# Last cross layer of the last 1024 rows with rows on partitions: column-tiled matmuls, sums added by identity matmuls, one multiply-add per 128 rows

## Chip, cores and metric

One core of a Trainium2 chip. The metric is the device time of one execution in microseconds (us). "Span" is the time from the first to the last instruction in a profile; the timed figure is some 1.75 us longer. Most runs agree within a few tenths; some are 1.5 to 2.5 us longer. Those over 1.5% above the kernel's fastest run are called slow and left out of ratios.

## The reference

```python
# x0: (4096, 416), ws: (6, 416, 416), bs: (6, 416), all bf16
x = x0
for l in range(6):
    x = x0 * (x @ ws[l] + bs[l]) + x
```

Since every layer adds onto x, x after layer l is x0 * (1 + sum of all (x @ ws + bs) so far). The kernel keeps this sum in PSUM and never resets it between the layers of one group of rows.

## The kernel before

Four superblocks of 1024 rows pass through six layers each. Features lie on partitions, rows on the free dimension. 416 features are three chunks of 128 and a tail of 32. TensorE works in four column tiles of 128x32 side by side for the chunks, and in row tiles for the tail. VectorE evicts each PSUM bank with one multiply:

```python
for half in range(2):            # 512 rows each
    ...
    for c in range(NC):          # three chunks of 128 features
        ...
        dve.scalar_tensor_tensor(
            out=dst, in0=ps[:, NC * half + c, :], scalar=cb_sb[:, c, l:l + 1],
            in1=x0T_sb[:, c, o:o + H], op0=ALU.add, op1=ALU.mult,
        ).then_inc((s_xa, s_xb)[half], 1)
```

`cb_sb` holds one plus the sum of biases, per feature. The result has features on partitions, but the output wants rows. Superblocks 0 to 2 are turned by DMA transposes, hidden behind the next superblock. The last one has nothing behind it, so it is turned on TensorE, copied by ScalarE and VectorE and stored in pieces; the last two stores (208 KB each) are released at the same moment:

```python
def out_chunk(c):                # first 512 rows: identity matmuls
    for j in range(4):
        for q in range(4):
            ins = tile_mm(ps[lane(q), c, j * 128:j * 128 + 128],
                xo_sb[:, NS - 1, c, j * 128 + 32 * q:j * 128 + 32 * q + 32], ident[:, :], q, True)
...
# rows 512 to 1023: transposes, then copies by VectorE and ScalarE
...
sp.wait_ge(s_oeD, 2)
sp.wait_ge(s_oet, 1)
sp.dma_start(out_v[:, j + 6:j + 8, :], o_sb[:, j + 6:j + 8, :]).then_inc(s_out, 16)
...
act.wait_ge(s_oet, 1)
act.wait_ge(s_oeA, 4)
act.wait_ge(s_oeD, 1)
act.dma_start(out_v[:, j0 + 4:j0 + 6, :], o_sb[:, j0 + 4:j0 + 6, :]).then_inc(s_out, 16)
```

## Time and profile before

| | |
|---|---|
| time | 131.05 us median of 3 runs (130.9 to 131.08) |
| span of the profiled run | 130.5 us, a slow run of 132.34 us |
| one layer of one superblock | 4.87 us |
| last VectorE copy to the end of the span | 3.17 us |

The page gives busy shares and the chain that ended last; the chain of waits in order of time shows the tail; the timeline gives durations. The prediction shows these lines.

### The profile page before, as it was taken

Reading aid. Unit: us, or ns where it says so; the run is one execution under the profiler, and the core shown is the slowest. Engines: PE = TensorE matmul, PEld = TensorE weight load, DVE = VectorE, ACT = ScalarE, POOL = GpSimd, SP = SyncE. Lnnn points to the kernel's source line nnn. Section 1 sums busy time; section 2 is a strip of 40 time slices with the busy share of each in tenths; the row PEclk is TensorE's granted clock in tenths of the full one; section 3 lists DMA queues with packets and bytes.
Section 4 is the critical chain, followed back from the end, with each engine's and each line's share of the span. In section 5 each row is a group of like instructions: output and inputs, shape, how many; then the busy total and the mean of one; then the engine's idle time right before and its main releaser. Section 6 shows DMA issues by size and latency. Waiting matters only on the chain.

```text
span 130.5 us, 5378 instructions
## 1 busy us (share of the span) xinstructions
PE 125.8 (96%) x2436; PEld 62.9 (48%) x2436; DVE 100.3 (77%) x154; ACT 71.5 (55%) x163; POOL 22.6 (17%) x41
## 2 busy tenths in 40 slices
PE   7999999999999999999999999999999999999980
PEld 5555445445445445445445445445445445445450
DVE  2427797797797797797798798798788788788780
ACT  0623563575763564575764564575754554554670
POOL 7502022022022023022022023022022023022140
PEclk9999999999999999999999999999999999999997
DMA  3963099900008979800006699700008900700026
GB/s 99 312 152 90 13 228 219 173 5 0 5 5 58 207 93 203 274 23 5 0 5 132 135 123 204 260 6 0 5 0 49 211 12 0 261 6 5 3 76 190
DMA packets 32882, 12.54 MB, mean 96 GB/s; under 512 B 25302, under 2 KB 32860, under 8 KB 32860
## 3 DMA queue, kind: packets, MB, share of 16 engines
q1 hardware_dynamic: 31356, 11.37, 42.9%
q10 hardware_dynamic: 1312, 0.78, 2.1%
q8 instruction: 19, 0.31, 1.0%
q0 software_dynamic: 192, 0.06, 0.2%
q14 instruction: 3, 0.02, 0.1%
HBM read 2.90 MB, written 3.41 MB: 48 GB/s over the span
## 4 chain that ended last, share of the span: by engine, by line
PE 93%; DMA 3%; DVE 1%; SPq 0%; issue 0%; DVEq 0%
PE ps L211 82%; PE ps L350 10%; DMA xin_sb<-in_x_dram 3%; PE ps L261 1%; DVE xo_sb L458 1%; DVE o_sb L463 0%; SPq L121 0%; DVEq L33 0%; PE ps L366 0%
## 5 line engine op out<-in xcount | busy, mean ns | idle before, releaser
L458 DVE SCALAR_TENSOR_TENSOR xT_sb<-ps,cb_sb,x0T_sb 128x512 bf16<-128x512 f32 x120 | 80.8, 743 | 16.6 <-PE ps L350 16.6
L211 PE MATMUL ps<-xT_sb,w_sb 128*32 128x512 bf16 (+1 forms) x1680 | 89.0, 364 | 0.0
L211 PEld LDWEIGHTS ps<-xT_sb,w_sb 128*32 128x32 bf16 x1680 | 43.0, 97 | 38.7 <-issue 4.2
L485 ACT ACTIVATE xt_sb<-xt_sb 32x256 bf16<-32x256 bf16 x80 | 33.1, 414 | 16.7 <-POOL xt_sb L198 16.0
L505 ACT ACTIVATE t_sb<-ps,cb_sb 64x256 f32<-64x256 f32 x48 | 22.5, 470 | 30.4 <-PE ps L211 30.1
L198 POOL TENSOR_TENSOR xt_sb<-t_sb,x0t_sb 128x256 bf16<-128x256 f32 x20 | 13.5, 674 | 85.9 <-ACT t_sb L505 85.9
L211 PE MATMUL ps<-x0T_sb,w_sb 128*32 128x512 bf16 (+1 forms) x336 | 19.8, 383 | 0.0
L458 DVE SCALAR_TENSOR_TENSOR xo_sb<-ps,cb_sb,x0T_sb 128x512 bf16<-128x512 f32 x23 | 15.6, 744 | 3.7 <-PE ps L350 3.3
L211 PEld LDWEIGHTS ps<-x0T_sb,w_sb 128*32 128x32 bf16 x336 | 8.9, 101 | 8.3 <-issue 2.1
L350 PE MATMUL ps<-xt_sb,wt_sb 32*128 32x512 bf16 x80 | 12.1, 379 | 0.0
L518 ACT ACTIVATE x0t_sb<-x_sb 32x256 bf16<-32x256 bf16 x24 | 9.9, 413 | 0.4
L366 PE MATMUL ps<-xt_sb,wt_sb 32*128 32x512 bf16 x40 | 7.8, 385 | 0.0
L350 PE MATMUL ps<-xt_sb,wc_sb 32*128 32x256 bf16 x80 | 7.7, 268 | 0.0
L350 PEld LDWEIGHTS ps<-xt_sb,wt_sb 32*128 32x128 bf16 x80 | 2.3, 92 | 8.5 <-DVE xT_sb L458 8.5
L350 PEld LDWEIGHTS ps<-xt_sb,wc_sb 32*128 32x128 bf16 x80 | 4.0, 93 | 2.3
L198 POOL TENSOR_TENSOR xot_sb<-t_sb,x0t_sb 128x256 bf16<-128x256 f32 x4 | 2.7, 674 | 12.6 <-ACT t_sb L505 12.6
L211 PE MATMUL ps<-const-bfloat16-1.0 128*32 128x256 bf16 x44 | 2.7, 416 | 0.8 <-PEq L556 0.8
L440 DVE CAST x0T_sb<-ps 128x256 bf16<-128x256 f32 x2 | 0.8, 425 | 3.2 <-PE ps L211 3.2
L480 ACT ACT_TABLE_LOAD x1 | 1.3, 1283 | 3.6 <-issue 3.6
L350 PE MATMUL ps<-x0t_sb,wt_sb 32*128 32x512 bf16 x16 | 2.4, 379 | 0.0
L489 ACT ACTIVATE x0t_sb<-ps 128x512 bf16<-128x512 f32 x1 | 0.6, 597 | 3.1 <-PE ps L211 3.1
L211 PEld LDWEIGHTS ps<-const-bfloat16-1.0 128*32 128x32 bf16 x44 | 1.8, 138 | 1.1 <-issue 0.8
(43 smaller groups left out, 32.0 us busy)
## 6 DMA issues: line engine op xcount, KB each, us to landing
out_dram<-o_sb SPq DMA_DIRECT2D x3, 832.0 KB, 4.1
w_sb<-in_ws_dram SPq DMA_DIRECT2D x5, 312.0 KB, 4.5
xin_sb<-in_x_dram SPq DMA_DIRECT2D x2, 208.0 KB, 3.7
w_sb<-in_ws_dram ACTq DMA_DIRECT2D x1, 312.0 KB, 3.8
out_dram<-o_sb SPq DMA_DIRECT2D x1, 256.0 KB, 2.7
xin_sb<-in_x_dram ACTq DMA_DIRECT2D x1, 208.0 KB, 2.8
out_dram<-o_sb SPq DMA_DIRECT2D x1, 208.0 KB, 2.2
out_dram<-o_sb ACTq DMA_DIRECT2D x1, 208.0 KB, 2.7
```

The lines of the kernel that those rows point to most:

```text
L198: pool.tensor_tensor(out=dst, in0=t32_sb[:, n % 2, :], in1=x0t_sb[:, s, 0:G], op=ALU.mult).then_inc(s_xt, 1)
L211: return pe.matmul(dst, lhsT=lhsT, rhs=rhs, start=start, stop=True, skip_group_check=True, tile_position=(0, 32 * q),)
L261: ins = pe.transpose(out=psT[:, IN_BANKS[h][c], (j % 2) * 128:(j % 2 + 1) * 128], in_=xin_sb[:, j, c * 128:(c + 1) * 128], identity=ident[ ...
L350: return pe.matmul(dst, lhsT=lhsT, rhs=srct[lane(g), cols], start=l == 0 and start, stop=True, skip_group_check=True, tile_position=(32 * ...
L366: pe.matmul(ps[:, NC * h + 2, :], lhsT=wt_sb[lane(g), l, 0:128], rhs=srct[lane(g), :].rearrange("p (b r) -> p b r", b=2)[:, ::-1, :], star ...
L440: dve.tensor_copy(out=x0T_sb[:, c, 512:768], in_=ps[:, THIRD[c], 0:G]).then_inc(s_inD, 1)
L458: dve.scalar_tensor_tensor(out=dst, in0=ps[:, NC * half + c, :], scalar=cb_sb[:, c, l:l + 1], in1=x0T_sb[:, c, o:o + H], op0=ALU.add, op1= ...
L480: act.activation(out=x0T_sb[:, 1, h * 256:(h + 1) * 256], in_=psT[:, IN_BANKS[h][1], 0:256], func=ACTF.Copy).then_inc(s_inA, 1)
L485: ins = act.activation(out=buf[lane(g), G:2 * G], in_=buf[lane(g ^ 1), 0:G], func=ACTF.Copy)
L489: act.activation(out=x0t_sb[:, 0, :], in_=ps[:, 5, :], func=ACTF.Copy).then_inc(s_te, 1)
L505: ins = act.activation(out=t32_sb[HALVES[h], n % 2, :], in_=tail(h), func=ACTF.Identity, bias=cb_sb[HALVES[h], NC, l:l + 1],)
L518: ins = act.activation(out=x0t_sb[lane(g), s + 1, swap * G:(swap + 1) * G], in_=x4_sb[96:128, s, r * G:(r + 1) * G], func=ACTF.Copy,)
```

## The change

Intent: compute the last layer of the last superblock directly with rows on partitions. The activations become the weights of the column tiles (32 rows each), and the layer's weight matrix streams through with 416 columns. No transpose and no copy is left at the end: one VectorE multiply-add per 128 rows writes the output tile. The price is that the sums of layers 0 to 4, which lie in PSUM the other way round, must be copied to bf16 and added by identity matmuls. Core of the diff, cut:

```diff
+            def nat_tile(t):
+                for k in range(NC):
+                    if k == 0 and t < 3:
+                        pe.wait_ge(s_xa, NC * (NL - 1))
+                        pe.wait_ge(s_q, t + 1)
+                    for q in range(4):
+                        tile_mm(
+                            ps[lane(q), NAT_BANKS[t], 0:D], xT_sb[:, (L - 1) % 2, k, t * 128 + 32 * q:t * 128 + 32 * q + 32],
+                            w_sb[:, L - 1, k, :], q, t < 3 and k == 0,
+                        )
+            def nat_sums(t):
+                ...      # 3 chunks x 4 column tiles: sums of the layers before, times the identity
+            nat_tile(0)
+            nat_tile(1)
+            pe.wait_ge(s_q, NC)
+            nat_sums(0)
+            nat_sums(1)
+            nat_tile(2)
+            nat_sums(2)
+            ...
             for r in range(2):
+                pe.wait_ge(s_xb, NC * (NL - 1) - (2, 0)[r])
+                pe.wait_ge(s_q, NC + 1 + r)
+                if r == 1:
+                    pe.wait_ge(s_qD, 1)
+                ...      # tail features: 4 row-tiled matmuls, 4 identity matmuls of 32 columns
+            ins.then_inc(s_nt, 3)
+            for t in range(3, JS):
+                nat_tile(t)
+                nat_sums(t).then_inc(s_nt, 1)
...
+            for t in range(JS):
+                dve.wait_ge(s_nt, max(t + 1, 3))
+                dve.scalar_tensor_tensor(
+                    out=o_sb[:, j0 + t, :], in0=ps[:, NAT_BANKS[t], 0:D], scalar=1.0,
+                    in1=x0n_sb[:, t, :], op0=ALU.add, op1=ALU.mult,
+                ).then_inc(s_o, 1)
...
+            for j in (2, 6):      # ScalarE's queue; (0, 4) on SyncE's
+                act.wait_ge(s_o, j + 2)
+                act.dma_start(out_v[:, j0 + j:j0 + j + 2, :], o_sb[:, j0 + j:j0 + j + 2, :]).then_inc(s_out, 16)
```

ScalarE makes five of the six bf16 copies of sums (`s_q` counts them), VectorE the last (`s_qD`), and POOL the tail's.

More of the change, by code (lines that the diff above doesn't have):

```diff
@@ L49, in bass_standalone__dcn_v2_cross__recsys_kernel @@
         t32_sb = sb("t32_sb", [128, 2, G], FP32)
-        a32_sb = sb("a32_sb", [128, H], FP32)
+        x0n_sb = sb("x0n_sb", [128, JS, D])
+        wl_sb = sb("wl_sb", [128, D])
         xo_sb = sb("xo_sb", [128, NS, NC, SB])
@@ L59, in bass_standalone__dcn_v2_cross__recsys_kernel @@
         cb_sb = sb("cb_sb", [128, NC + 1, L], FP32)
+        cq_sb = sb("cq_sb", [128, NC + 2], FP32)
         ps = es.enter_context(nc.psum_tensor("ps", [128, 8, 512], FP32))
@@ L77, in bass_standalone__dcn_v2_cross__recsys_kernel @@
         s_xa, s_xb = sem("s_xa"), sem("s_xb")
-        s_a32, s_xaP = sem("s_a32"), sem("s_xaP")
+        s_cq, s_q, s_qD, s_qt = sem("s_cq"), sem("s_q"), sem("s_qD"), sem("s_qt")
+        s_x0n, s_wl, s_nt = sem("s_x0n"), sem("s_wl"), sem("s_nt")
         s_ta, s_xt, s_sw = sem("s_ta"), sem("s_xt"), sem("s_sw")
         s_oT, s_ot, s_otc = sem("s_oT"), sem("s_ot"), sem("s_otc")
-        s_pA, s_pB, s_pt, s_out = sem("s_pA"), sem("s_pB"), sem("s_pt"), sem("s_out")
-        s_oet, s_oeA, s_oeD = sem("s_oet"), sem("s_oeA"), sem("s_oeD")
+        s_out, s_o = sem("s_out"), sem("s_o")
         x0_v = x0.rearrange("(j p) d -> p j d", p=128)
@@ L96, in bass_standalone__dcn_v2_cross__recsys_kernel @@
         THIRD = (3, 6, 7)
+        NAT_BANKS = (0, 1, 2, 6, 7, 4, 3, 5)
         HALVES = (slice(0, 64), slice(64, 128))
@@ L103, in tail @@
             return ps[HALVES[h], 6 + h, 0:G]
+        j0 = (NS - 1) * JS
         def load_wt(eng, g, a, b, done):
@@ L145, in _ @@
                     load_rows(s + 2)
+                if s == 0:
+                    for g in range(4):
+                        sp.dma_start(wl_sb[lane(g), :], ws[L - 1, DF:D, :]).then_inc(s_wl, 16)
+                if s == 1:
+                    sp.dma_start(x0n_sb[:, :, :], x0_v[:, (NS - 1) * JS:NS * JS, :]).then_inc(s_x0n, 16)
                 sp.wait_ge(s_oT, 16 * NC * (s + 1))
@@ L150, in _ @@
                 ).then_inc(s_out, 16)
-            j = (NS - 1) * JS
-            sp.wait_ge(s_oeA, 2)
-            sp.dma_start(out_v[:, j:j + 4, 0:256], o_sb[:, j:j + 4, 0:256]).then_inc(s_out, 16)
-            sp.wait_ge(s_oeA, 3)
-            sp.wait_ge(s_oet, 1)
-            sp.dma_start(out_v[:, j:j + 4, 256:D], o_sb[:, j:j + 4, 256:D]).then_inc(s_out, 16)
-            sp.wait_ge(s_oeD, 2)
-            sp.wait_ge(s_oet, 1)
-            sp.dma_start(out_v[:, j + 6:j + 8, :], o_sb[:, j + 6:j + 8, :]).then_inc(s_out, 16)
+            for j in (0, 4):
+                sp.wait_ge(s_o, j + 2)
+                sp.dma_start(
+                    out_v[:, j0 + j:j0 + j + 2, :], o_sb[:, j0 + j:j0 + j + 2, :]
+                ).then_inc(s_out, 16)
             sp.wait_ge(s_out, 16 * (NS + 3))
@@ L191, in _ @@
                     if n == NL:
-                        pool.wait_ge(s_a32, 1)
+                        break
+                    if n == 1:
+                        pool.tensor_scalar(
+                            out=cq_sb[:, 0:NC + 1], in0=cb_sb[:, :, L - 1], scalar1=-1.0, scalar2=None, op0=ALU.add
+                        ).then_inc(s_cq, 1)
+                        pool.wait_ge(s_cq, 1)
                         pool.tensor_tensor(
-                            out=xo_sb[:, s, 2, 0:H], in0=a32_sb[:, :], in1=x0T_sb[:, 2, s * SB:s * SB + H], op=ALU.mult
-                        ).then_inc(s_xaP, 1)
+                            out=cq_sb[:, NC + 1:NC + 2], in0=cq_sb[:, NC:NC + 1], in1=cb_sb[:, NC, L - 2:L - 1], op=ALU.subtract
+                        ).then_inc(s_cq, 1)
                     pool.wait_ge(s_ta, n)
@@ L200, in _ @@
                     ).then_inc(s_xt, 1)
+                    if n == NL - 1:
+                        pool.tensor_scalar(
+                            out=xot_sb[:, s, :], in0=t32_sb[:, n % 2, :], scalar1=cq_sb[:, NC + 1:NC + 2], scalar2=None, op0=ALU.add
+                        ).then_inc(s_qt, 1)
                     if l == 2 and s > 0:
@@ L265, in _ @@
                 ins.then_inc(s_inT, 1)
-            def out_chunk(c):
-                for j in range(4):
-                    for q in range(4):
-                        ins = tile_mm(
-                            ps[lane(q), c, j * 128:j * 128 + 128],
-                            xo_sb[:, NS - 1, c, j * 128 + 32 * q:j * 128 + 32 * q + 32], ident[:, :], q, True,
-                        )
-                ins.then_inc(s_pA, 1)
             for s in range(NS):
@@ L278, in _ @@
                     n = s * L + l
-                    last = n == NL - 1
+                    if n == NL - 1:
+                        break
                     if l == 0:
@@ L388, in _ @@
                         chunk(m, 1).then_inc(s_mb, 1)
-                        if last and m < 2:
-                            pe.wait_ge(s_xa, NC * (NL - 1) + m + 1)
-                            out_chunk(m)
-                            if m == 1:
-                                pe.wait_ge(s_xaP, 1)
-                                out_chunk(2)
-            pe.wait_ge(s_xt, NL)
-            pe.wait_ge(s_xb, NC * NL - 2)
-            for r in range(2):
-                for q in range(4):
-                    c = r * 128 + 32 * q
-                    ins = tile_mm(ps[lane(q), 3, r * 128:r * 128 + 128], xot_sb[:, NS - 1, c:c + 32], ident[:, :], q, True)
@@ L402, in _ @@
-            ins.then_inc(s_pt, 1)
-            def out_transposes(c, j, bank, slot):
-                return pe.transpose(
-                    out=psT[:, bank, slot * 128:(slot + 1) * 128],
-                    in_=xo_sb[:, NS - 1, c, j * 128:(j + 1) * 128], identity=ident[:, :],
-                )
-            pe.wait_ge(s_xb, NC * NL - 1)
-            for jj in range(4):
-                for c in range(2):
-                    ins = out_transposes(c, 4 + jj, 4, jj * 2 + c)
-            ins.then_inc(s_pB, 1)
@@ L415, in _ @@
-            pe.wait_ge(s_xb, NC * NL)
-            pe.wait_ge(s_oeA, 1)
-            for jj in range(4):
-                ins = out_transposes(2, 4 + jj, (5, 0)[jj // 2], jj % 2)
-                if jj % 2:
-                    ins.then_inc(s_pB, 1)
-        j0 = (NS - 1) * JS
+            def nat_tile(t):
[8 more added lines that the diff above has]
+                        )
@@ new lines, in nat_sums @@
+            def nat_sums(t):
+                for c in range(NC):
+                    for q in range(4):
+                        ins = tile_mm(
+                            ps[lane(q), NAT_BANKS[t], c * 128:c * 128 + 128],
+                            xo_sb[:, NS - 1, c, t * 128 + 32 * q:t * 128 + 32 * q + 32], ident[:, :], q, False,
+                        )
+                return ins
+            nat_tile(0)
+            nat_tile(1)
+            pe.wait_ge(s_q, NC)
+            nat_sums(0)
@@ new lines, in _ @@
+            nat_sums(1)
+            nat_tile(2)
+            nat_sums(2)
+            pe.wait_ge(s_xt, NL - 1)
+            pe.wait_ge(s_qt, 1)
+            pe.wait_ge(s_wl, 64)
+            for r in range(2):
+                pe.wait_ge(s_xb, NC * (NL - 1) - (2, 0)[r])
+                pe.wait_ge(s_q, NC + 1 + r)
+                if r == 1:
+                    pe.wait_ge(s_qD, 1)
+                for g in range(4):
+                    t, rows = 2 * g + r, slice(r * 128, r * 128 + 128)
+                    pe.matmul(
+                        ps[:, NAT_BANKS[t], 0:D], lhsT=xt_sb[lane(g), (L - 1) % 2, rows], rhs=wl_sb[lane(g), :],
+                        start=t >= 3, stop=True, skip_group_check=True, tile_position=(32 * g, 0),
+                    )
+                for g in range(4):
+                    t, rows = 2 * g + r, slice(r * 128, r * 128 + 128)
+                    ins = pe.matmul(
+                        ps[:, NAT_BANKS[t], DF:D], lhsT=xot_sb[lane(g), NS - 1, rows], rhs=ident[lane(g), lane(g)],
+                        start=False, stop=True, skip_group_check=True, tile_position=(32 * g, 0),
+                    )
@@ L444, in _ @@
                     n = s * L + l
+                    if n == NL - 1:
+                        break
                     for half in range(2):
@@ L447, in _ @@
                             dve.wait_ge(s_ti, n + 1)
-                        for c in range(NC):
-                            if n == NL - 1 and half == 0 and c == 2:
-                                continue
+                        for c in (1, 0, 2) if n == NL - 2 and half == 0 else range(NC):
+                            if n == NL - 2 and half == 0 and c == 0:
+                                dve.wait_ge(s_q, 1)
                             if half == 1:
@@ L461, in _ @@
                             ).then_inc((s_xa, s_xb)[half], 1)
-            dve.wait_ge(s_pB, 1)
-            dve.tensor_copy(
-                out=o_sb[:, j0 + 4:j0 + 8, 0:256], in_=psT[:, 4, :].rearrange("p (j d) -> p j d", d=256)
-            ).then_inc(s_oeD, 1)
-            dve.wait_ge(s_pB, 3)
-            dve.tensor_copy(
-                out=o_sb[:, j0 + 6:j0 + 8, 256:DF], in_=psT[:, 0, 0:256].rearrange("p (j d) -> p j d", d=128)
-            ).then_inc(s_oeD, 1)
+            dve.wait_ge(s_cq, 1)
+            dve.tensor_scalar(
+                out=xo_sb[:, NS - 1, 2, H:SB], in0=ps[:, NC + 2, :], scalar1=cq_sb[:, 2:3], scalar2=None, op0=ALU.add
+            ).then_inc(s_qD, 1)
+            dve.wait_ge(s_x0n, 16)
+            for t in range(JS):
[4 more added lines that the diff above has]
+                ).then_inc(s_o, 1)
         @block.scalar
@@ L486, in swap_lanes, with previous_sums @@
                 ins.then_inc(done, 1)
+            def previous_sums(half, c):
+                act.activation(
+                    out=xo_sb[:, NS - 1, c, half * H:(half + 1) * H], in_=ps[:, NC * half + c, :],
+                    func=ACTF.Identity, bias=cq_sb[:, c:c + 1],
+                ).then_inc(s_q, 1)
             act.wait_ge(s_tp, 1)
@@ L496, in _ @@
                     if n == NL:
+                        break
+                    if n == NL - 1:
+                        act.wait_ge(s_cq, 1)
                         act.wait_ge(s_ti, n)
-                        act.activation(
-                            out=a32_sb[:, :], in_=ps[:, 2, :], func=ACTF.Identity, bias=cb_sb[:, 2, l:l + 1],
-                        ).then_inc(s_a32, 1)
+                        previous_sums(0, 0)
+                        act.wait_ge(s_xa, NC * (n - 1) + 1)
+                        previous_sums(0, 1)
                     act.wait_ge(s_to, n)
@@ L509, in _ @@
                     ins.then_inc(s_ta, 1)
-                    if l < L - 1:
+                    if n == NL - 1:
+                        act.wait_ge(s_xa, NC * n)
+                        previous_sums(0, 2)
+                        for c in range(2):
+                            act.wait_ge(s_xb, NC * (n - 1) + c + 1)
+                            previous_sums(1, c)
+                    elif l < L - 1:
                         act.wait_ge(s_xt, n)
@@ L523, in _ @@
                             ins.then_inc(s_te, 1)
-            for c in range(NC):
-                act.wait_ge(s_pA, c + 1)
-                act.activation(
-                    out=o_sb[:, j0:j0 + 4, c * 128:c * 128 + 128],
-                    in_=ps[:, c, :].rearrange("p (j d) -> p j d", d=128), func=ACTF.Copy,
-                ).then_inc(s_oeA, 1)
-            act.wait_ge(s_pt, 1)
-            act.activation(
-                out=o_sb[:, j0:j0 + JS, DF:D].rearrange("p (g r) f -> p r g f", r=2),
-                in_=ps[:, 3, 0:256].rearrange("p (r g f) -> p r g f", g=4, f=DR), func=ACTF.Copy,
-            ).then_inc(s_oet, 1)
-            act.wait_ge(s_pB, 2)
-            act.activation(
-                out=o_sb[:, j0 + 4:j0 + 6, 256:DF], in_=psT[:, 5, 0:256].rearrange("p (j d) -> p j d", d=128), func=ACTF.Copy
-            ).then_inc(s_oeA, 1)
-            act.wait_ge(s_oet, 1)
-            act.wait_ge(s_oeA, 4)
-            act.wait_ge(s_oeD, 1)
-            act.dma_start(out_v[:, j0 + 4:j0 + 6, :], o_sb[:, j0 + 4:j0 + 6, :]).then_inc(s_out, 16)
+            for j in (2, 6):
+                act.wait_ge(s_o, j + 2)
+                act.dma_start(
+                    out_v[:, j0 + j:j0 + j + 2, :], o_sb[:, j0 + j:j0 + j + 2, :]
+                ).then_inc(s_out, 16)
 _INS = ['x0', 'ws', 'bs']
```

## The prediction

> **What bounds the kernel now.** I read the page first: busy shares, then the chain that ended last.
>
> ```profile
> PE 125.8 (96%) x2436; PEld 62.9 (48%) x2436; DVE 100.3 (77%) x154; ACT 71.5 (55%) x163; POOL 22.6 (17%) x41
> ...
> PE 93%; DMA 3%; DVE 1%; SPq 0%; issue 0%; DVEq 0%
> ```
>
> TensorE carries 93% of the chain. The change touches only the end, so next I took the chain of waits from 100 us on, in order of time. Columns: start, length, what.
>
> ```profile
> 117.21 0.32 PE ps L350
> ...
> 117.76 4.33 PE ps L211 x84
> 122.08 0.32 PE ps L350
> ...
> 122.63 3.13 PE ps L211 x96
> 125.76 0.03 issue
> 125.79 0.75 DVE xo_sb L458
> 126.54 0.60 DVE o_sb L463
> 127.14 0.20 DVEq L33
> ```
>
> One layer of one superblock is 122.08 - 117.21 = 4.87 us. The last layer follows: TensorE until 125.76, one VectorE multiply, copies, and the stores. The span ends at 130.5, so 3.1 us after the last copy are DMA and the end of the program. Then the timeline of these stretches:
>
> ```profile
> 117.83 4.04 DVE L458 SCALAR_TENSOR_TENSOR xT_sb<-ps,cb_sb,x0T_sb 128x512 bf16<-128x512 f32 x6 [0.83 <-PE ps L350]
> 118.25 0.95 ACT L505 ACTIVATE t_sb<-ps,cb_sb 64x256 f32<-64x256 f32 x2 [1.44 <-PE ps L211]
> 119.28 0.68 POOL L198 TENSOR_TENSOR xt_sb<-t_sb,x0t_sb 128x256 bf16<-128x256 f32 x1 [4.19 <-ACT t_sb L505]
> ...
> 122.70 0.69 ACT L498 ACTIVATE a_sb<-ps,cb_sb 128x512 f32<-128x512 f32 x1 [1.02 <-PE ps L350]
> ...
> 123.55 0.40 PE L211 MATMUL ps<-ident,xo_sb 128*32 128x128 bf16 x16
> ...
> 123.77 0.82 PE L211 MATMUL ps<-xT_sb,w_sb 128*32 128x512 bf16 x12
> ...
> 124.42 0.67 PE L211 MATMUL ps<-ident,xo_sb 128*32 128x128 bf16 x32
> ...
> 127.36 0.37 SPq L159 DMA_DIRECT2D out_dram<-o_sb  x1
> 127.37 0.46 ACTq L542 DMA_DIRECT2D out_dram<-o_sb  x1
> ```
>
> Three rates come from here. Six VectorE evictions of 128x512 take 4.04 us and one lasts 0.743, so they start (4.04 - 0.743)/5 = 0.66 us apart. Twelve 512-column matmuls (three groups of four column tiles side by side) go from 123.77 to 124.42: 0.217 us a group. Sixteen identity matmuls of 128 columns go from 123.55 to 123.77: 0.055 us a group of four.
>
> **What the Trainium skill says.** "TensorE: Matmul & The Clock Gate", section "Wait — 56ns, not 53.3ns?", gives N/2.4 + 2.5 ns between warm matmuls: 215.7 at 512 and 55.6 at 128 columns. The trace agrees for groups of four (217 and 55), so I use the same form for 416 columns: 176 ns, an estimate. "TensorEngine Tiling (Array Packing)", "Key Properties", says that a change of tiling mode drains TensorE. In the trace a layer streams 18 x 0.216 + 3 x 0.109 + 2 x 0.216 = 4.65 us of its 4.87, so two switches cost about 0.22, 0.11 each. The same page, "PSUM Bottleneck", warns that tiling does not speed up the emptying of PSUM; that is the rival I end up believing. "DMA: Bandwidth & Descriptors", "Anatomy of one DMA", puts a transfer at about 2.0 us fixed plus bytes over 436 GB/s, 2.5 us for 208 KB. The section is about another issue path; here the page's list of DMA issues shows 2.2 and 2.7 us for the two last stores of 208 KB, which were in flight together.
>
> **The change part by part.** Superblock 3, layer 5 no longer produces features on partitions. Removed, all after 120.1 us: 72 matmuls of 512, 12 of 256 and the row-tiled tail matmuls; 5 VectorE multiplies of 0.66 and two copies; 48 + 8 identity matmuls, 12 transposes; ScalarE's five evictions and POOL's 1.16 us multiply. Added: per 128 rows, 12 matmuls of 416 columns and 12 identity matmuls of 128; two row-tiled tail groups; five ScalarE and one VectorE copies of the sums of the layers before into bf16; eight VectorE multiply-adds of 128x416. The loads of x0 rows (832 KB) and of the weights' last rows are queued while superblocks 0 and 1 end, over 50 us before their use: hidden.
>
> TensorE, on the old clock. The second half of layer 4 ends 9 groups before 122.08: 122.08 - 9 x 0.216 = 120.14. A new row tile costs 3 x 0.176 = 0.53, its sums 3 x 0.056 = 0.17. Tiles 0 and 1 run to 121.20, their sums to 121.53, tile 2 with sums to 122.23. The gates are met early enough. ScalarE's copies are each about 0.69 (as the a_sb row). Copy 0 goes 117.83 to 118.52; copy 1 must wait for VectorE's first eviction and ends near 119.3; the two tail evictions (0.95) end at 120.25; copy 2 ends at 120.9, before TensorE asks for it at 121.20; copies 3 and 4 end by 122.2. POOL's multiply ends near 121.0, its added op by 121.7. The first tail group (switch 0.11, stream 0.176, 32-column sums about 0.03) ends at 122.55.
>
> The second tail group is the first true wait. It needs VectorE's own copy of the last bank, which stands behind six evictions: 117.83 + 4.04 + 0.66 = 122.53. From an eviction's end to the first dependent matmul the trace shows 0.11 (123.44 to 123.55): 122.64. The group streams 0.21, to 122.85, and drains about 0.17 (a 128-column matmul is shown as 0.220 long and streams 0.056); VectorE answers 0.07 later: 123.09.
>
> Now two engines run beside each other. **TensorE**: switch 0.11 and five tiles of 0.695 end at 126.44, with drain 126.6. **VectorE**: a multiply-add of 416 columns should be 96 elements shorter than the old one; at 0.96 GHz (one fp32 PSUM element per cycle, the skill's "VectorE: DVE Perf Modes", "Why PSUM operands drop a tier"; the 0.66 spacing for 512 is above that floor of 0.533) this is 0.10 less: 0.56 apart, 0.643 long. Eight take 7 x 0.56 + 0.643 = 4.56: from 123.09 to 127.65. If only TensorE bound, the last would end at 126.6 + 0.07 + 0.643 = 127.31. So VectorE ends it, by 0.34.
>
> The last store (ScalarE's queue, 208 KB) is issued 0.03 later. The one before it was released two multiply-adds, 1.1 us, earlier, so it shares less than now; I choose 2.3 us to landing, between 2.2 and 2.7. The old last store landed at 127.37 + 2.7 = 130.07, 0.43 before the span's end; that stays. Sum: 127.65 + 0.03 + 2.3 + 0.43 = 130.41 against 130.50. The timed 131.05 less 0.09 is 130.96; I say 130.9, because the new multiply-add takes an immediate instead of a per-partition scalar and may be a little shorter.
>
> So the expected gain is almost nothing: transposes and copies at the end go away, but the eight multiply-adds, which cannot start before 123.09, take their place one for one.
>
> **The rivals.** (a) TensorE binds the tail, because VectorE's new form is quicker than 0.56 apart: for it speaks that the two are within 0.34 us; then 127.3 for the last multiply, about 130.6 in time. (b) The early part slips: ScalarE's chain of copies is late, since each waits for VectorE to leave the bank, and TensorE stalls at the sums of tile 0 or at the second tail group. Slack is 0.3 us in the first place and 0.4 in the second; a slip of one 0.69 copy would add some 0.3, about 131.3. Against it: every duration is in the trace. (c) The stores decide: four even stores of 208 KB, released pairwise 1.1 us apart, no longer collide, and the last lands in 2.0, about 130.6; or ScalarE's queue is slower by itself and it stays 2.7, about 131.3. The data of the two old stores moved at some 340 GB/s together, which speaks for the shorter time. (d) TensorE pays more for the swapped operands, a new weight block of 32 columns for each 416-column matmul. Against: the old stream also loads one per matmul and the loads are only 48% busy. If it took 0.80 per tile instead of 0.695, the last tile would come 0.5 later and the time would be 131.2.
>
> **Range and chances.** These move the result by 0.3 to 0.5 us each and can add up: 130.0 to 131.9 should hold it 8 times in 10. A change by 2% is 2.6 us; the whole tail after 123.09 is 7.4 us, and no rival takes a third of it. Faster by over 2%: 0.03; within 2%: 0.93; slower: 0.04.
>
> **What would show it.** Right: in the changed profile the eight multiply-adds stand back to back, some 4.5 us in one row, begin near 123.1, and end near 127.6; the wait before them is TensorE's, which itself waited for VectorE's copy; the chain names VectorE for about 5 us in place of TensorE; TensorE ends before 127. Wrong: gaps between the multiply-adds that TensorE ends (rival a or d), an idle stretch of TensorE before 122.5 (b), a last store of other than 2.0 to 2.7 us (c), or any layer period before 117 us that is no longer 4.87, which would mean that the early loads or the two small POOL ops are not free.

## The result

The changed kernel took 129.97 us median (129.86 to 132.36, 4 runs, one of them slow) against 130.98 for the kernel before (4 runs). The ratio is 0.9924, 95% interval 0.9902 to 0.9947. Ratios here are the mean time of one kernel's fast runs over that of the other's of the same rounds, so not quite the ratio of the quoted medians. The change is within 2%, as forecast, but 129.97 lies just under the range's low end of 130.0, and the gain is about 1.0 where 0.09 to 0.15 was expected.

The changed kernel's page, span, busy shares and chain:

```profile
span 128.3 us, 5471 instructions
PE 124.1 (97%) x2482; PEld 62.7 (49%) x2482; DVE 100.7 (79%) x156; ACT 68.9 (54%) x156; POOL 22.2 (17%) x42
...
PE 90%; DVE 6%; ACT 1%; issue 0%; DVEq 0%; ACTq 0%
```

VectorE took 6% of the chain in place of 1%. The end of its chain of waits (start, length, what):

```profile
116.28 0.70 ACT xo_sb L520
116.98 0.02 issue
117.00 3.38 DVE xT_sb L486 x5
120.39 0.67 DVE xo_sb L491
121.05 0.14 issue
121.19 0.35 PE ps L435 x2
121.54 0.07 PE ps L441 x3
...
121.70 4.09 DVE o_sb L497 x8
```

This is the predicted order: six evictions, VectorE's copy of the last sums (L491), the second tail group, then eight multiply-adds in one row. Its timeline, with the idle time before an entry in brackets:

```profile
115.54 0.39 PE L358 MATMUL ps<-xt_sb,wt_sb 32*128 32x512 bf16 x1
...
116.22 4.16 DVE L486 SCALAR_TENSOR_TENSOR xT_sb<-ps,cb_sb,x0T_sb 128x512 bf16<-128x512 f32 x6 [0.83 <-PE ps L358]
...
121.70 4.09 DVE L497 SCALAR_TENSOR_TENSOR o_sb<-ps,x0n_sb 128x416 bf16<-128x416 f32 x8 [0.66 <-PE ps L441]
...
122.82 2.37 SPq L164 DMA_DIRECT2D out_dram<-o_sb  x2
123.82 2.41 ACTq L572 DMA_DIRECT2D out_dram<-o_sb  x2
...
124.81 0.34 PE L227 MATMUL ps<-ident,xo_sb 128*32 128x128 bf16 x12
```

Two things differ from the plan. The multiply-adds take 4.09, not 4.56. And everything in this profile stands 1.61 us earlier than in the first profile of before: the first tail matmul of the last layer but one (layer 4 of superblock 3) is at 115.54 here and was at 117.15 there. That difference exists already at the very first tail matmul, 8.37 against 9.97. From the first tail matmul to that of the last layer but one there are 107.17 and 107.18 us. So the spans of these two profiles must not be compared as they are. What can be compared is the stretch from the first tail matmul of the last layer but one to the end of the span; I call it **the tail**:

| | before | after |
|---|---|---|
| tail | 130.5 - 117.15 = 13.35 | 128.3 - 115.54 = 12.76 |
| of it, to the end of the last VectorE op | 127.33 - 117.15 = 10.18 | 125.79 - 115.54 = 10.25 |
| of it, from there to the end (stores) | 3.17 | 2.51 |

The tail is 0.59 shorter, and none of that is computing: the compute part is 0.07 longer and the stores' part 0.66 shorter. The lists of DMA issues, with the size and the us to landing (from the issue until all data have arrived), of before (from 120 us on):

```profile
out_dram<-o_sb SPq DMA_DIRECT2D x1, 208.0 KB, 2.2
out_dram<-o_sb ACTq DMA_DIRECT2D x1, 208.0 KB, 2.7
```

and of the changed kernel:

```profile
out_dram<-o_sb SPq DMA_DIRECT2D x2, 208.0 KB, 2.1
out_dram<-o_sb ACTq DMA_DIRECT2D x2, 208.0 KB, 2.1
```

Theory: the gain comes from the stores, which no longer leave together; the end is bound by VectorE and TensorE about equally. Rivals: the start became shorter; VectorE alone bounds the end; the stores don't matter.

### The profile page after: what moved, and what is told of

It is laid out like the page before. It is cut to its first block, busy times and chain, and to the rows that moved or that the text cites. A ratio compares the mean times of both kernels' runs of the same rounds, so it can differ in the third digit from the quotient of the medians.

```text
span 128.3 us, 5471 instructions
## 1 busy us (share of the span) xinstructions
PE 124.1 (97%) x2482; PEld 62.7 (49%) x2482; DVE 100.7 (79%) x156; ACT 68.9 (54%) x156; POOL 22.2 (17%) x42
## 4 chain that ended last, share of the span: by engine, by line
PE 90%; DVE 6%; ACT 1%; issue 0%; DVEq 0%; ACTq 0%
PE ps L227 79%; PE ps L358 10%; DVE o_sb L497 3%; DVE xT_sb L486 3%; PE ps L277 1%; ACT xo_sb L520 1%; DVE xo_sb L491 1%; PE ps L435 0%; PE ps L374 0%; PE ps L441 0%; DVEq L496 0%; ACTq L537 0%
## 5 line engine op out<-in xcount | busy, mean ns | idle before, releaser
L227 PE MATMUL ps<-xT_sb,w_sb 128*32 128x512 bf16 (+1 forms) x1596 | 84.2, 364 | 0.0
L227 PEld LDWEIGHTS ps<-xT_sb,w_sb 128*32 128x32 bf16 x1596 | 40.9, 97 | 37.2 <-issue 4.0
L516 ACT ACTIVATE xt_sb<-xt_sb 32x256 bf16<-32x256 bf16 x76 | 31.5, 414 | 15.8 <-POOL xt_sb L210 15.1
L545 ACT ACTIVATE t_sb<-ps,cb_sb 64x256 f32<-64x256 f32 x46 | 21.6, 469 | 28.6 <-PE ps L227 28.3
L486 DVE SCALAR_TENSOR_TENSOR xo_sb<-ps,cb_sb,x0T_sb 128x512 bf16<-128x512 f32 x18 | 12.1, 744 | 2.5 <-PE ps L358 2.5
L358 PE MATMUL ps<-xt_sb,wt_sb 32*128 32x512 bf16 x76 | 11.5, 379 | 0.0
L374 PE MATMUL ps<-xt_sb,wt_sb 32*128 32x512 bf16 x38 | 7.4, 385 | 0.0
L227 PE MATMUL ps<-w_sb,xT_sb 128*32 128x416 bf16 x96 | 5.4, 340 | 0.0
L497 DVE SCALAR_TENSOR_TENSOR o_sb<-ps,x0n_sb 128x416 bf16<-128x416 f32 x8 | 4.1, 584 | 0.7 <-PE ps L441 0.7
L520 ACT ACTIVATE xo_sb<-ps,cq_sb 128x512 bf16<-128x512 f32 x5 | 3.3, 685 | 1.1 <-PE ps L358 1.1
L227 PEld LDWEIGHTS ps<-w_sb,xT_sb 128*32 128x32 bf16 x96 | 2.1, 96 | 1.3 <-DVE xT_sb L486 0.4
```

The lines of the kernel that those rows point to most:

```text
L227: return pe.matmul(dst, lhsT=lhsT, rhs=rhs, start=start, stop=True, skip_group_check=True, tile_position=(0, 32 * q),)
L358: return pe.matmul(dst, lhsT=lhsT, rhs=srct[lane(g), cols], start=l == 0 and start, stop=True, skip_group_check=True, tile_position=(32 * ...
L374: pe.matmul(ps[:, NC * h + 2, :], lhsT=wt_sb[lane(g), l, 0:128], rhs=srct[lane(g), :].rearrange("p (b r) -> p b r", b=2)[:, ::-1, :], star ...
L486: dve.scalar_tensor_tensor(out=dst, in0=ps[:, NC * half + c, :], scalar=cb_sb[:, c, l:l + 1], in1=x0T_sb[:, c, o:o + H], op0=ALU.add, op1= ...
L497: dve.scalar_tensor_tensor(out=o_sb[:, j0 + t, :], in0=ps[:, NAT_BANKS[t], 0:D], scalar=1.0, in1=x0n_sb[:, t, :], op0=ALU.add, op1=ALU.mul ...
L516: ins = act.activation(out=buf[lane(g), G:2 * G], in_=buf[lane(g ^ 1), 0:G], func=ACTF.Copy)
```

## The experiments

The tail of every profile (spans are given to 0.1, so the tail is good to about 0.05). Each edited kernel has a single profile:

| run | first tail matmul | last layer but one | span | tail |
|---|---|---|---|---|
| before, first profile (slow) | 9.97 | 117.15 | 130.5 | 13.35 |
| before again | 8.02 | 115.20 | 128.7 | 13.50 |
| before, third profile | 8.49 | 115.67 | 129.0 | 13.33 |
| after | 8.37 | 115.54 | 128.3 | 12.76 |
| after again, twice | 8.77, 8.06 | 115.94, 115.24 | 128.7, 128.0 | 12.76, 12.76 |
| scalar per partition | 8.65 | 115.82 | 129.0 | 13.18 |
| stores together | 8.06 | 115.24 | 128.6 | 13.36 |
| before, one last store | 8.53 | 115.71 | 128.5 | 12.79 |
| VectorE told earlier | 8.48 | 115.66 | 128.4 | 12.74 |
| no sums | 8.16 | 115.33 | 128.1 | 12.77 |
| both of these | 8.21 | 115.38 | 127.6 | 12.22 |
| last store small | 8.16 | 115.34 | 127.7 | 12.36 |
| combined (slow) | 9.83 | 117.01 | 129.1 | 12.09 |

Between the second and third column lie 107.17 or 107.18 us in every row, so the loads that the change adds lengthened no layer. Nearly all run-to-run variation sits ahead of the first tail matmul (the tail of before itself ranged over 13.33 to 13.50), so the tail can be compared even where a profile fell in a slow run.

### Is the start part of the gain?

No edit: the kernel before, profiled again.

> The unchanged kernel before, for a profile in the fast state. In the first profile the first tail matmuls start at 9.97 us and the span is 130.5; in the changed kernel's they start at 8.36. Theory A (the first profile of before fell in the slow state and only its start was late): the first tail matmuls start near 8.4 to 8.8, the layers stay 4.87 apart, and the span is near 129.2; from the first tail matmul of the last layer but one (117.15 in the first profile) to the end of the span stays 13.35. Theory B (the change itself shortened the start): they start near 10.0 again and the span stays 130.5.

> The kernel before unedited, a third profile. The stretch from the first tail matmul of the last layer but one to the end was 13.35 and 13.5 in two profiles; the changed kernel's is 12.76 in three. If the change's gain lies in that stretch alone, this one is again 13.3 to 13.5 and the first tail matmuls start within the changed kernel's 8.06 to 8.77 when the run is fast. If the change also moves the start, they start later than 8.8 in a fast run.

Measured: starts of 8.02 and 8.49, spans of 128.7 and 129.0, tails of 13.50 and 13.33 (each a single run, 130.39 and 130.71 us; both times lie within the kernel's fast runs, 130.38 to 131.47 in the largest set). Theory A holds in the main: the late start of 9.97 belonged to that run, not to the kernel. Its numbers were hit only roughly: one start is earlier than I expected, and the tail of 13.50 is 0.15 longer than 13.35, because the last store landed in 2.8 there. What differs between the slow start and the early one is the speed of the first matmuls. The timeline of the slow first profile:

```profile
5.52 2.75 PE L211 MATMUL ps<-x0T_sb,w_sb 128*32 128x512 bf16 x24
```

and of the second profile of the same kernel:

```profile
5.27 1.48 PE L211 MATMUL ps<-x0T_sb,w_sb 128*32 128x512 bf16 x24
```

In the slow one the weight loads of the groups come at 5.90, 6.33, 6.75 and 7.18, so 0.43 apart, twice the 0.216 of later groups. The Trainium skill ("TensorE: Matmul & The Clock Gate", "Part 1: The HAM clock gate") says that the array starts at 1.2 GHz and is released by an activity window that runs free, so that the release varies from run to run; 512 columns at 1.2 GHz are 0.427. The trace agrees with that number. Its clock records say more: the first record of full granted clock begins at 9.31 us in the slow profile, at 8.95 in the combined version's (also a slow run, with a start of 9.83), and between 3.87 and 6.65 in the twelve others. (`prof` shows a PEclk of 1.00 in all of these stretches, because nothing is recorded ahead of that first record.) A late clock is not the only cause of a late start: in the run with the start of 8.77 the full clock was there at 3.87, but TensorE waited 0.97 us for the load of `xtl_sb`. The changed kernel's own slow run (132.36 against 129.9 to 130.0) was not profiled.

### The base on the other chips

No edit: the changed kernel again.

> The changed kernel unedited, as the base of the other runs of this chip. Expected 129.9 to 130.1 and a span of 128.2 to 128.4, eight multiply-adds in 4.09 us.

> The changed kernel unedited again, as the base of this chip and for more fast runs against the kernel before: the stretch from the first tail matmul of the last layer but one to the end stays at 12.76, and the ratio of the times lies near 0.995, since 13.35 to 13.5 less 12.76 is 0.6 to 0.7 us of 131, while starts vary by some 0.4 from run to run.

Measured: medians 130.35 (130.06 to 131.84, 4 runs) and 130.05 (129.69 to 130.35, 6 runs); ratios 0.9963 (0.9869 to 1.0057) and 0.9932 (0.9903 to 0.9961). The tail was 12.76 both times and the multiply-adds took 4.09 both times. The first median lay above the expected 130.1; in the profiled run (130.53) the start was late, 8.77, and the other three runs were not profiled.

### Immediate or per-partition scalar

```diff
-                    out=o_sb[:, j0 + t, :], in0=ps[:, NAT_BANKS[t], 0:D], scalar=1.0,
+                    out=o_sb[:, j0 + t, :], in0=ps[:, NAT_BANKS[t], 0:D], scalar=nc.const_aps.tensor_like(1.0, cb_sb[:, 0, 0:1]),
```

> The eight multiply-adds take a per-partition scalar of 1.0 in place of an immediate. If the scalar's form is why they stand 0.50 us apart and not 0.56 as predicted, they last 0.64 each and eight take 4.5 us, and the time rises by 0.4 (130.4). If the form of the scalar costs nothing, eight stay at 4.1 and the time stays at 130.0.

The tile view of `o_sb` (count, then ns min/median/max) in this run:

```profile
L497 DVE SCALAR_TENSOR_TENSOR o_sb<-ps,const-float32-1.0,x0n_sb x8: 643/643/652, 122.0 to 125.9; 128x416 bf16<-128x416 f32 x8
```

and in the changed kernel:

```profile
L497 DVE SCALAR_TENSOR_TENSOR o_sb<-ps,x0n_sb x8: 581/581/593, 121.7 to 125.2; 128x416 bf16<-128x416 f32 x8
```

Measured: 643 against 581 ns, 62 for each; the timeline has 4.56 for eight in place of 4.09, and the tail grew by 0.42 to 13.18. The time, 130.64 (130.24 to 131.98), is 0.3 above the base's 130.35 on this chip, though with this spread that alone would prove nothing. The 4.56 is exactly the prediction's figure: its duration was right for a per-partition scalar, and the kernel uses an immediate.

### Stores together

```diff
             for j in (0, 4):
-                sp.wait_ge(s_o, j + 2)
+                sp.wait_ge(s_o, j + 2 if j == 0 else JS)
```

> The store of tiles 4 and 5 is held back until all eight tiles are done, so that it goes out with the store of tiles 6 and 7, as two stores of 208 KB did in the kernel before. If the gain of the change comes from its staggered stores (rival c of the prediction), the time rises by 0.5 to 0.65 to about 130.5 or 130.6, the last landing takes 2.6 or 2.7 in place of 2.1, and the multiply-adds stay as they are. If the stores don't matter, it stays at 130.0.

The tile view of `o_sb`, landing times of the four stores:

```profile
DMA to landing us min/median/max: 2.0/2.1/2.7
```

Measured: the longest landing is 2.7 again (2.2 was the longest in the changed kernel), the multiply-adds stay at 4.09, and the tail is 13.36, that of the kernel before. The timed median was 130.45 (130.29 to 131.0), only 0.1 above the base: this profile's start was 0.7 earlier than the base's (8.06 against 8.77), and four runs each don't average that out. So the expected rise of the time was not seen in the clocked runs; it was seen in the trace.

A likely reason, which no run tests by itself: while the data of these two stores move, the DMA engines carry 342 to 363 GB/s in the full slices of the DMA view, and the last store of the changed kernel alone also reaches 354. At 355 GB/s 208 KB take 0.60 us (an estimate from these rates), so the data of one store would hold up those of the other by about that much.

### The kernel before with one last store

Wrong on purpose: the last store on ScalarE's queue is left out.

```diff
-            act.wait_ge(s_oet, 1)
-            act.wait_ge(s_oeA, 4)
-            act.wait_ge(s_oeD, 1)
-            act.dma_start(out_v[:, j0 + 4:j0 + 6, :], o_sb[:, j0 + 4:j0 + 6, :]).then_inc(s_out, 16)
```

> The kernel before, wrong on purpose: its last store on ScalarE's queue (208 KB) is left out, so the other last store goes alone. In the kernel before the stretch from the first tail matmul of the last layer but one to the end is 13.35 and 13.5 in two profiles. If two stores side by side cost what staggered stores save, the remaining one lands in 2.1 instead of 2.2 to 2.4, and the stretch falls by 0.5 to 0.65 to about 12.8 to 12.9. If the stores don't matter, it stays above 13.3.

The list of DMA issues:

```profile
out_dram<-o_sb SPq DMA_DIRECT2D x1, 208.0 KB, 2.1
```

Measured (one run): the remaining last store landed in 2.1, and the tail fell to 12.79. Seen from both sides, two stores of 208 KB released at once lengthen the tail by 0.60 (changed kernel) and by 0.54 to 0.71 (kernel before, by the profile that is taken). The change shortens it by 0.57 to 0.74, so this is its gain in the tail.

### Which engine bounds the tail?

Three runs, each timed and profiled once. First, VectorE is told after the first tail group, and takes tile 2 before tile 1; SyncE's first store therefore waits for one tile more:

```diff
-                sp.wait_ge(s_o, j + 2)
+                sp.wait_ge(s_o, j + 2 + (j == 0))
...
-            ins.then_inc(s_nt, 3)
+                ins.then_inc(s_nt, 1)
...
-            for t in range(JS):
-                dve.wait_ge(s_nt, max(t + 1, 3))
+            for t in (0, 2, 1, 3, 4, 5, 6, 7):
+                dve.wait_ge(s_nt, {0: 1, 2: 1, 1: 2}.get(t, t))
```

> TensorE tells VectorE after the first tail group already that tiles 0 and 2 are complete, so VectorE need not wait for the second tail group. From the first tail matmul of the last layer but one to the end the changed kernel takes 12.76 us. If VectorE alone bounds the tail, as the prediction had it, the multiply-adds start 0.6 earlier and that stretch falls to about 12.2. If TensorE bounds it as well (its last matmul ends at 125.15, the last multiply-add starts at 125.20), it stays at 12.7 to 12.8 and gaps show between the multiply-adds that TensorE ends.

Second, TensorE is relieved of the identity matmuls of tiles 3 to 7:

```diff
                for q in range(4):          # in nat_tile
-                        tile_mm(
+                        ins = tile_mm(
...
+                return ins
...
             for t in range(3, JS):
-                nat_tile(t)
-                nat_sums(t).then_inc(s_nt, 1)
+                nat_tile(t).then_inc(s_nt, 1)
```

> Wrong on purpose: the identity matmuls of tiles 3 to 7 are left out, 5 x 0.167 = 0.83 us of TensorE. If VectorE bounds the tail as well, TensorE ends 0.8 earlier and the stretch to the end stays at 12.7 to 12.8. If TensorE alone bounds it, the stretch falls towards 12.0.

Third, both edits together, so again with a wrong output:

> Wrong on purpose: both edits together, VectorE told after the first tail group and no identity matmuls for tiles 3 to 7. If the two engines bound the tail together, this one gains what neither gains alone: eight multiply-adds back to back from about 0.6 earlier, and a stretch of about 12.15. If something else holds the end, it stays near 12.7.

Measured tails: 12.74, 12.77 and 12.22. Neither edit gains anything, the two together 0.54. The end of the chain of waits in the first of them:

```profile
121.31 0.35 PE ps L435 x2
121.65 0.03 PE ps L441 x3
121.68 3.62 PE ps L227 x120
125.30 0.02 issue
125.32 0.59 DVE o_sb L497
```

VectorE began at 121.30, but its eight multiply-adds took 4.61, with gaps that TensorE's last tiles ended: the chain runs over TensorE for 3.62. In the third run the chain ends in multiply-adds without gaps, from 0.5 earlier:

```profile
121.03 3.57 DVE o_sb L497 x7
```

So in the changed kernel TensorE and VectorE bound the end together. A slower multiply-add costs nearly its full amount there (0.42 of 0.47 in the scalar experiment); that a faster one would gain nothing follows from this, but was not run.

### A smaller last store

```diff
-            for j in (2, 6):
-                act.wait_ge(s_o, j + 2)
+            for a, b in ((2, 4), (7, 8)):
+                act.wait_ge(s_o, b)
...
+            sp.wait_ge(s_o, JS - 1)
+            sp.dma_start(out_v[:, j0 + 6:j0 + 7, :], o_sb[:, j0 + 6:j0 + 7, :]).then_inc(s_out, 16)
```

> The changed kernel with only its last stores split: tile 6 goes out as soon as it is complete, tile 7 alone as the last store of 104 KB. If the landing's length depends on the bytes (208 KB moved in about 0.6 us), the last landing takes about 1.8 in place of 2.1 and the stretch falls to about 12.5. If it is nearly all fixed, it stays above 12.65.

The list of DMA issues:

```profile
out_dram<-o_sb SPq DMA_DIRECT2D x1, 104.0 KB, 1.9
out_dram<-o_sb ACTq DMA_DIRECT2D x1, 104.0 KB, 1.7
```

Measured: the last store lands in 1.7 in place of 2.1 and the tail is 12.36, 0.40 shorter, more than the expected 0.25. The time is 129.82 (129.48 to 131.92, one of 6 runs slow), ratio to before 0.9916 (0.9885 to 0.9948); the intervals of this run and of its base overlap, so of the times alone one would not call it faster.

### All of it together

VectorE told earlier and the small last store as above; besides, VectorE evicts the first half's banks in another order, and one step of tile 3 runs ahead of the tail groups (`start` is set there in turn):

```diff
-                        for c in (1, 0, 2) if n == NL - 2 and half == 0 else range(NC):
+                        for c in (1, 2, 0) if n == NL - 2 and half == 0 else range(NC):
...
             nat_sums(2)
+            nat_tile(3, (0,))
...
-                nat_tile(t)
+                nat_tile(t, (1, 2) if t == 3 else range(NC))
```

> A version meant to be faster than both. Four edits to the changed kernel: VectorE is told after the first tail group; it takes the banks of the first half in the order 1, 2, 0, so it need not wait 0.1 for ScalarE's first copy; the first three-row-group step of tile 3 (0.18 of TensorE) runs ahead of the tail groups, in what was a wait of about 0.25; the last two tiles are stored one by one (104 KB each). If TensorE and VectorE bound the tail together and the landing depends on the size, the stretch from the first tail matmul of the last layer but one to the end falls from 12.76 by 0.1 + 0.15 + 0.2 to about 12.3, and the time is 0.4 to 0.5 below the changed kernel's. If the edits of the two engines give nothing because a third thing holds them, only the store's part remains, 12.55.

Measured: the output is correct, 129.06 us median (128.83 to 130.91, 6 runs, one slow), ratio to the kernel before 0.9861 (0.9830 to 0.9892); the base has 0.9932 (0.9903 to 0.9961), so this version beats both kernels, by less than 2%: the two intervals do not overlap. In its profile (the slow run) the evictions of the last layer but one take 4.04 again instead of 4.16 and the multiply-adds begin 5.71 after the first tail matmul of that layer, instead of 6.16:

```profile
117.69 4.04 DVE L489 SCALAR_TENSOR_TENSOR xT_sb<-ps,cb_sb,x0T_sb 128x512 bf16<-128x512 f32 x6 [0.83 <-PE ps L360]
...
122.72 4.25 DVE L500 SCALAR_TENSOR_TENSOR o_sb<-ps,x0n_sb 128x416 bf16<-128x416 f32 x8 [0.33 <-PE ps L444]
```

The tail is 12.09: of the 0.67 less than 12.76, 0.29 is computing (the last multiply-add ends 9.96 after that matmul instead of 10.25) and 0.38 is the store. The 0.46 that I expected had the store at 0.2.

## Why the prediction was right or wrong

What failed are two sizes in the sum and what followed from one of them: the multiply-add (0.643 long, measured 0.581), the landing of the last store (2.3, measured 2.1), and the conclusion that VectorE alone ends the tail. Against the kernel before, the gain in the tail lies in the stores; against the prediction, the larger miss is the multiply-adds.

- **TensorE's stream, right.** The estimate of 0.176 for a group of 416 columns and 0.056 for sums gives 0.695 a tile; in the changed kernel's timeline the tiles from 122.20 on start 0.69 to 0.70 apart. TensorE's last matmul ends at 125.15, 9.61 after the first tail matmul of the last layer but one; predicted were 126.6 - 117.15 = 9.45. Rival (d) is out.
- **The first true wait, right, 0.22 late.** Multiply-adds were to start 123.09 - 117.15 = 5.94 after that matmul and started 6.16 after it. Of this 0.12 is the evictions, 4.16 instead of 4.04: bank 0 must wait for ScalarE's first copy, which the working had placed beside VectorE without a cost. The combined run, with another order, gets the 4.04 back. The other 0.1 is spread over hand-overs between the engines: from VectorE's copy to the second tail group 0.15 instead of 0.11, the rest around that group. The slip of rival (b), a late copy of ScalarE that holds TensorE at the sums, did not occur.
- **The step "0.56 apart, 0.643 long", wrong.** They are 0.50 apart and 0.581 long; eight take 4.09 instead of 4.56. The working subtracted 96 elements from the old multiply but kept the old form's per-partition scalar; it is worth 62 ns per instruction, as the scalar experiment shows. The prediction named the immediate as a possibility and gave it 0.06 us in all, where it was 0.47.
- **The step "So VectorE ends it, by 0.34", wrong in consequence.** With the shorter multiply-adds and the later start TensorE and VectorE end together; the last multiply-add starts at 125.20, 0.05 after TensorE's end. Rival (a) is half true.
- **"One for one", right, with some luck.** Last VectorE op against last VectorE op, the compute part of the tail is 10.25 against 10.18: the multiply-adds did take the place of transposes and copies. By the working it should have been 127.65 - 117.15 = 10.50; the late start (0.22) hid part of the 0.47 by which the multiply-adds were shorter.
- **The step "I choose 2.3 us to landing", mis-sized.** The last store landed in 2.1 and the span ended 2.51 after the last multiply-add, where the sum had 0.03 + 2.3 + 0.43 = 2.76. This is rival (c), which the prediction put at 130.6: the stores no longer leave together. Two experiments, one on each kernel, show it as 0.54 to 0.71. Its other half, that ScalarE's queue is slower by itself, is out: the last store of the changed kernel is on that queue, alone, and landed in 2.1.
- **The sum.** Predicted tail: 130.41 - 117.15 = 13.26; measured 12.76, so 0.50 too long: 0.22 too early at the start of the multiply-adds, 0.47 too long in them, 0.25 too long in the store. On these terms the gain should have been 13.35 - 12.76 = 0.59, and the time about 130.4, inside the range.
- **The rest, not settled.** The first call measured a gain of 1.0, the third (10 fast runs of before, 6 of after) a ratio of 0.9932, which is 0.9; the second 0.9963, 0.5. The tail explains 0.57 to 0.74, depending on which profile of before is taken. The fast runs of all three together average 130.98 (20 of before) and 130.20 (13 of after), 0.78 apart, which leaves 0.04 to 0.21. Fast starts ranged over 8.02 to 8.77 whatever the kernel, which is enough to move the mean of three or four runs by some tenths, and I take the remainder for that; it is not shown. I have only two profiles of the kernel before without the late start, so a small real difference in the start can't be excluded. Also, the range's low end of 130.0 left nothing for this scatter.
- **The first profile's state.** I read a span of 130.5 beside a time of 131.05 and took them as one run. The page belonged to a run of 132.34. It did no harm to the differences, because the late start shifts everything, but it hid that the starts vary.
- **Slips without consequence.** 130.5 - 127.34 is 3.2, not 3.1. ScalarE loses eight activations of the last layer, not five, and POOL a second multiply of 0.67. Rival (d) comes to 131.1 by its own sum, because VectorE's 0.34 takes up part of the 0.5. The chain names VectorE for 8.1 us (3.38 + 0.67 + 4.09), not about 5, because it runs back through five evictions as well.

## What to carry to other kernels

At the end of a kernel, look at what is released last and in which company: stores that leave together land later, so let the pieces become ready in turn and make the last one small. When one kind of last stage replaces another, compare the new chain with the old from a common point late in the trace; here this resolved tenths that the timed runs could not. Before scaling a duration from an old row to a new instruction, check that the operand forms are the same, not only the shapes.

## What the Trainium skill lacked or had wrong

- "VectorE: DVE Perf Modes", "Scalar operands", names the immediate and the per-partition scalar as two forms but gives no difference in time, nor does another page for VectorE. Here the form with a per-partition scalar took 643 ns and the one with an immediate 581, for 128x416 from fp32 PSUM.
- "DMA: Bandwidth & Descriptors", "Anatomy of one DMA", fits 2.0 us plus bytes over 436 GB/s, for another issue path; by that fit 208 KB would be an estimate of 2.5 us, 104 KB of 2.2. Stores from SyncE's and ScalarE's queues landed in 2.1 and 1.7 to 1.9 here, and the skill has no such fit for them. Nor does it give a time for what two stores released together cost each other: 2.7 instead of 2.1 for the later one.
- "TensorE: Matmul & The Clock Gate", "Part 1: The HAM clock gate", puts the start's penalty under 1% of a typical kernel. Here the two profiles with a late full clock (8.95 and 9.31 us) start at 9.83 and 9.97, the others at 8.02 to 8.77. That is 1.1 to 2.0 us, 0.8 to 1.5% of 130, for the difference between runs alone, and more than the change itself gained.
